# A gated recurrence with a causal gated unit: one store per chunk, and transfers in a searched order

## The chip, the cores and the metric

The kernel runs on one core of a Trainium2 chip. The metric is device time in microseconds (us), the median of the runs. The core has five engines with an instruction stream each: TensorE (PE), VectorE (DVE), ScalarE (ACT), GpSimd (POOL) and SyncE (SP, which here only issues loads). Sixteen DMA engines move data between HBM and the on-chip memory SBUF.

## The reference

The input has 4 sequences of 6336 tokens with 256 channels, in float32. A recurrence runs over the tokens, and its output feeds a gated unit whose gate is a causal convolution of 5 taps.

```python
# recurrence, c = 8
a_base = sigmoid(a_param)
a_t    = exp(c * sigmoid(r_gate) * log(clip(a_base, 1e-6, 1 - 1e-6)))
x_gated = sqrt(maximum(1 - a_t * a_t, 1e-6)) * sigmoid(i_gate) * x
for t in range(S):
    h = a_t[:, t] * h + x_gated[:, t]
    y[:, t] = h
# gated unit on y
gate_pre = sum over k of conv_w[k] * (y shifted by 4 - k tokens)
out = (sigmoid(gate_pre) * (y @ w_val)) @ w_out
```

x, r_gate, i_gate and the output have 26 MB each.

## The kernel before

The 25344 tokens are cut into 27 chunks, most of 1024 tokens (the first and two late ones 512, the last 256). For the convolution and what follows, a chunk is cut again into halves of 512. Each step of a chunk is a small function, and the text PLAN lists the steps in the order in which they are emitted, as name.chunk.half.PSUM-bank. Every engine executes its own steps in that order.

```python
NRI = 3     # buffers for the gates r and i
NX = 2      # buffers for x
NOSB = 5    # output buffers, half a chunk each
X_PE = [0, 1]   # chunks whose x goes through PE and DVE rather than POOL

PLAN = """
ldri.0.-1 ldri.1.-1 ldx.0.-1 ldx.1.-1 ldri.2.-1 ldw.-1 tanh.0.-1 srT.0.0.7 srT.0.1.5 exp.0.1.-1 exp.0.0.-1 e.0.0.-1
...
"""

def op_ldri(k, bank):                 # loads of both gates, on SP
    for e, src in ((0, rf), (1, if_)):
        nc.sync.dma_start(gate[:, slot(c, e), 0:n * H]..., toks(src, c, 0, n))
def op_ldx(k, bank):
    nc.sync.dma_start(xr[:, c % NX, 0:CHUNKS[c] // P, :], toks(xf, c, 0, CHUNKS[c]))
def op_tanh(k, bank):                 # ACT, both gates in one instruction, in place
    nc.scalar.activation(out=tgate[:, s0:s0 + 2, 0:w], in_=gate[:, s0:s0 + 2, 0:w], func=ACT.Tanh, scale=0.5)
# op_srT: PE transposes tanh(r/2); op_exp: ACT, a = exp(khf * t + khf) into aring
def op_e(k, bank):                    # POOL: a * a into ering
    nc.gpsimd.tensor_tensor(out=ering[...], in0=a, in1=a, op=ALU.mult)
def op_s1(k, bank):                   # POOL: 1 + tanh(i/2), in place in the i gate's buffer
    nc.gpsimd.tensor_scalar(out=t, in0=t, scalar1=1.0, scalar2=1.0, op0=ALU.add, op1=ALU.mult)
def op_u(k, bank):                    # POOL: u = (1 + tanh(i/2)) * x
    if c in X_PE: return op_ux(...)   # or on DVE, with x copied to PSUM by PE (op_xc)
    nc.gpsimd.tensor_tensor(out=u, in0=t, in1=xt, op=ALU.mult)
# op_sq: ACT, sqrt over one to three chunks, with another activation table
# op_nT: PE transposes the root; op_xg: DVE, u * root; op_xgT: PE transposes it
# op_scan: DVE, the recurrence; op_conv: PE, 5 taps; op_tg: ACT, tanh of the convolution
# op_val: PE, y @ w_val
def op_gv(k, bank):                   # DVE: (1 + tanh) * val
    nc.vector.scalar_tensor_tensor(out=gvr[:, nth[k] % NGV, :, 0:n], in0=tgr[...], scalar=1.0, in1=..., ...)
# op_out: PE, gv @ w_out into PSUM
def op_osbA(k, bank): nc.scalar.copy(out=dst, in_=src)            # PSUM to osb, on ACT
def op_osbD(k, bank): nc.vector.tensor_copy(out=dst, in_=src)     # or on DVE
def op_store(k, bank):                # one store per half chunk (512 KB), issued by ACT
    nc.scalar.dma_start(toks(of, c, o, n), osb[:, nth[k] % NOSB, 0:n // P * D]...)
```

DMAs signal completion through eight semaphores that the framework hands out in turn. A new transfer on a semaphore waits for the transfer that used it before.

Of the kernel before, what the change touches and what calls it, by code (L numbers as in the profile page):

```python
# [16 lines left out]
X_PE = [0, 1]  # L17
NRI = 3
NX = 2
# [4 lines left out]
NOSB = 5  # L24
NTG = 2
NGV = 2
# [7 lines left out]
ldri.0.-1 ldri.1.-1 ldx.0.-1 ldx.1.-1 ldri.2.-1 ldw.-1 tanh.0.-1 srT.0.0.7 srT.0.1.5 exp.0.1.-1 exp.0.0.-1 e.0.0.-1  # L34
tanh.1.-1 e.0.1.-1 xc.0.1.0 xc.0.0.6 ux.0.0.-1 xc.1.2.1 u.0.-1 sq.0.1.-1 ux.1.2.-1 srT.1.0.0 ldri.3.-1 xc.1.1.5
ldx.2.-1 nT.0.0.7 srT.1.1.4 exp.1.0.-1 xg.0.0.-1 ux.1.1.-1 exp.1.1.-1 xc.1.0.0 tanh.2.-1 xc.1.3.5 e.1.1.-1 ux.1.0.-1
e.1.0.-1 wc.-1 srT.2.0.3 s1.2.-1 srT.2.1.2 xgT.0.0.4 exp.2.0.-1 scan.0.0.-1 exp.2.1.-1 e.2.0.-1 u.1.-1 tanh.3.-1
ldx.3.-1 ldri.4.-1 e.2.1.-1 u.2.-1 srT.3.1.3 srT.3.0.6 xgT.0.1.1 sq.1.2.-1 s1.3.-1 ldx.4.-1 ldri.5.-1 nT.2.0.7
nT.2.1.0 u.3.-1 xg.2.0.-1 exp.3.1.-1 xg.2.1.-1 nT.1.1.7 scan.0.1.-1 nT.1.0.5 tanh.4.-1 xg.1.1.-1 conv.0.0.0 xg.1.0.-1
xgT.2.0.3 e.3.1.-1 ldx.5.-1 xgT.1.1.4 ldri.6.-1 xgT.1.0.2 scan.1.1.-1 tg.0.0.-1 exp.3.0.-1 s1.4.-1 srT.4.1.1  # L40
exp.4.1.-1 scan.1.0.-1 val.0.0.4 e.3.0.-1 tanh.5.-1 srT.4.0.6 gv.0.0.-1 conv.1.0.0 u.4.-1 scan.2.0.-1 xgT.2.1.7
tg.1.0.-1 srT.5.1.5 srT.5.0.4 exp.4.0.-1 scan.2.1.-1 val.1.0.0 exp.5.1.-1 e.4.1.-1 ldx.6.-1 ldri.7.-1 exp.5.0.-1
gv.1.0.-1 conv.2.0.6 tanh.6.-1 e.5.1.-1 out.0.0.4 conv.1.1.0 osbD.0.0.-1 e.4.0.-1 val.2.0.2 tg.1.1.-1 val.1.1.4
e.5.0.-1 store.0.0.-1 tg.2.0.-1 out.1.0.0 conv.2.1.6 osbD.1.0.-1 s1.5.-1 sq.3.3.-1 gv.1.1.-1 u.5.-1 gv.2.0.-1
out.2.0.0 out.1.1.4 osbD.2.0.-1 osbD.1.1.-1 s1.6.-1 nT.3.1.3 ldri.8.-1 nT.3.0.2 ldx.7.-1 val.2.1.0 tg.2.1.-1 xg.3.0.-1
xg.3.1.-1 store.1.0.-1 u.6.-1 tanh.7.-1 gv.2.1.-1 xgT.3.1.7 nT.4.0.6 scan.3.1.-1 srT.6.0.1 srT.6.1.4 xgT.3.0.2
nT.4.1.0 nT.5.1.5 exp.6.0.-1 xg.4.0.-1 s1.7.-1 ldri.9.-1 xg.4.1.-1 exp.6.1.-1 srT.7.0.1 xg.5.1.-1 ldx.8.-1 nT.5.0.6
scan.3.0.-1 exp.7.0.-1 out.2.1.4 e.6.1.-1 tanh.8.-1 xgT.4.1.3 srT.7.1.7 xg.5.0.-1 conv.3.0.0 e.7.0.-1 osbD.2.1.-1
scan.4.1.-1 conv.3.1.4 u.7.-1 store.1.1.-1 tg.3.0.-1 xgT.4.0.6 srT.8.0.2 tg.3.1.-1 scan.4.0.-1 srT.8.1.0 exp.7.1.-1
val.3.1.4 exp.8.1.-1 gv.3.1.-1 e.6.0.-1 conv.4.1.6 ldx.9.-1 exp.8.0.-1 ldri.10.-1 xgT.5.0.3 store.2.0.-1 tg.4.1.-1  # L50
out.3.1.4 e.7.1.-1 scan.5.0.-1 tanh.9.-1 xgT.5.1.7 val.3.0.0 e.8.0.-1 conv.4.0.2 gv.3.0.-1 osbD.3.1.-1 e.8.1.-1
tg.4.0.-1 scan.5.1.-1 val.4.1.4 s1.8.-1 val.4.0.0 sq.6.3.-1 out.3.0.2 gv.4.1.-1 u.8.-1 gv.4.0.-1 osbD.3.0.-1 out.4.0.0
out.4.1.2 osbD.4.0.-1 srT.9.1.6 osbD.4.1.-1 nT.8.1.5 s1.9.-1 ldri.11.-1 nT.6.1.4 xg.8.1.-1 exp.9.1.-1 conv.5.0.2
ldx.10.-1 xg.6.1.-1 store.3.0.-1 tanh.10.-1 e.9.1.-1 nT.6.0.4 nT.7.1.1 xg.6.0.-1 nT.7.0.0 xgT.6.1.5 xg.7.0.-1 u.9.-1
xgT.6.0.4 xg.7.1.-1 srT.9.0.6 scan.6.0.-1 nT.8.0.7 exp.9.0.-1 conv.5.1.0 tg.5.0.-1 scan.6.1.-1 tg.5.1.-1 xgT.7.1.2
s1.10.-1 ldri.12.-1 store.2.1.-1 tanh.11.-1 val.5.1.0 ldx.11.-1 xg.8.0.-1 srT.10.1.3 srT.10.0.6 gv.5.1.-1 e.9.0.-1
val.5.0.4 conv.6.1.0 gv.5.0.-1 exp.10.1.-1 u.10.-1 srT.11.1.7 scan.7.1.-1 store.3.1.-1 store.4.1.-1 conv.6.0.4
tg.6.1.-1 exp.10.0.-1 srT.11.0.1 xgT.7.0.0 tg.6.0.-1 val.6.0.2 scan.7.0.-1 exp.11.0.-1 e.10.0.-1 out.5.0.4 ldri.13.-1
store.4.0.-1 ldx.12.-1 exp.11.1.-1 osbD.5.0.-1 out.5.1.0 e.10.1.-1 tanh.12.-1 conv.7.0.6 osbD.5.1.-1 e.11.0.-1
val.6.1.4 gv.6.0.-1 gv.6.1.-1 out.6.0.2 tg.7.0.-1 e.11.1.-1 store.5.1.-1 osbD.6.0.-1 xgT.8.1.6 xgT.8.0.7 s1.11.-1  # L60
out.6.1.4 scan.8.1.-1 sq.9.3.-1 val.7.0.2 u.11.-1 gv.7.0.-1 osbD.6.1.-1 conv.7.1.2 scan.8.0.-1 srT.12.0.1 srT.12.1.6
nT.9.0.0 nT.9.1.4 s1.12.-1 ldri.14.-1 nT.11.0.5 xg.9.0.-1 exp.12.0.-1 nT.10.0.7 ldx.13.-1 xg.9.1.-1 store.6.1.-1
xg.11.0.-1 store.5.0.-1 tg.7.1.-1 xgT.9.1.0 e.12.0.-1 scan.9.1.-1 exp.12.1.-1 out.7.0.2 tanh.13.-1 val.7.1.4 u.12.-1
osbD.7.0.-1 conv.8.0.0 gv.7.1.-1 nT.10.1.2 xgT.9.0.3 xg.10.1.-1 tg.8.0.-1 srT.13.0.6 scan.9.0.-1 s1.13.-1 ldri.15.-1
store.7.0.-1 tanh.14.-1 val.8.0.0 ldx.14.-1 out.7.1.4 xg.10.0.-1 e.12.1.-1 conv.8.1.2 gv.8.0.-1 srT.13.1.7 osbD.7.1.-1
store.6.0.-1 tg.8.1.-1 u.13.-1 xgT.10.0.1 srT.14.0.0 scan.10.0.-1 exp.13.0.-1 srT.14.1.4 out.8.0.2 exp.14.0.-1
xgT.10.1.6 store.7.1.-1 osbD.8.0.-1 exp.13.1.-1 conv.9.0.0 e.14.0.-1 exp.14.1.-1 scan.10.1.-1 ldx.15.-1 val.8.1.2
ldri.16.-1 tg.9.0.-1 nT.11.1.7 val.9.0.4 e.13.0.-1 store.8.0.-1 tanh.15.-1 gv.8.1.-1 conv.9.1.0 gv.9.0.-1 e.14.1.-1
out.8.1.2 val.9.1.4 osbD.8.1.-1 tg.9.1.-1 e.13.1.-1 xg.11.1.-1 store.8.1.-1 gv.9.1.-1 xgT.11.0.3 out.9.0.0 s1.14.-1
sq.12.3.-1 scan.11.0.-1 out.9.1.6 xgT.11.1.5 u.14.-1 osbD.9.1.-1 osbD.9.0.-1 val.10.0.6 srT.15.1.4 scan.11.1.-1  # L70
conv.10.0.2 s1.15.-1 nT.12.1.1 ldri.17.-1 tg.10.0.-1 nT.12.0.0 xg.12.1.-1 ldx.16.-1 srT.15.0.5 exp.15.1.-1 xg.12.0.-1
conv.10.1.2 gv.10.0.-1 u.15.-1 exp.15.0.-1 xgT.12.0.0 val.10.1.6 scan.12.0.-1 tg.10.1.-1 nT.13.1.1 store.9.0.-1
tanh.16.-1 conv.11.0.4 gv.10.1.-1 nT.13.0.3 e.15.0.-1 ldri.18.-1 nT.14.0.0 xg.13.1.-1 out.10.1.6 ldx.17.-1 xg.14.0.-1
xg.13.0.-1 tg.11.0.-1 e.15.1.-1 srT.16.0.2 osbD.10.1.-1 out.10.0.0 tanh.17.-1 val.11.0.6 osbD.10.0.-1 s1.16.-1
xgT.12.1.3 gv.11.0.-1 srT.16.1.1 conv.11.1.4 u.16.-1 scan.12.1.-1 exp.16.1.-1 val.11.1.6 tg.11.1.-1 srT.17.1.0
exp.16.0.-1 gv.11.1.-1 xgT.13.0.5 srT.17.0.4 store.10.0.-1 exp.17.1.-1 conv.12.0.2 scan.13.0.-1 e.16.0.-1 ldri.19.-1
store.9.1.-1 exp.17.0.-1 nT.14.1.0 ldx.18.-1 xgT.13.1.7 tg.12.0.-1 xg.14.1.-1 e.17.1.-1 scan.13.1.-1 store.10.1.-1
tanh.18.-1 out.11.0.2 xgT.14.0.4 e.16.1.-1 conv.12.1.0 osbD.11.0.-1 val.12.1.6 scan.14.0.-1 e.17.0.-1 tg.12.1.-1
out.11.1.2 val.12.0.0 s1.17.-1 gv.12.1.-1 sq.15.3.-1 gv.12.0.-1 out.12.1.6 u.17.-1 osbD.11.1.-1 out.12.0.4
osbD.12.1.-1 xgT.14.1.2 val.13.0.0 osbD.12.0.-1 conv.13.0.6 scan.14.1.-1 s1.18.-1 srT.18.0.3 ldri.20.-1 srT.18.1.5  # L80
tg.13.0.-1 nT.16.1.4 ldx.19.-1 store.12.0.-1 exp.18.1.-1 nT.17.0.2 gv.13.0.-1 u.18.-1 conv.13.1.6 store.11.0.-1
store.11.1.-1 exp.18.0.-1 xg.16.1.-1 nT.15.1.5 xg.17.0.-1 nT.15.0.1 tg.13.1.-1 xg.15.1.-1 val.13.1.2 xg.15.0.-1
tanh.19.-1 out.13.0.4 gv.13.1.-1 e.18.1.-1 ldri.21.-1 xgT.15.0.1 osbD.13.0.-1 conv.14.0.6 ldx.20.-1 scan.15.0.-1
e.18.0.-1 store.12.1.-1 tg.14.0.-1 srT.19.0.5 nT.17.1.0 exp.19.0.-1 nT.16.0.7 s1.19.-1 val.14.0.2 xg.17.1.-1
tanh.20.-1 xg.16.0.-1 xgT.15.1.5 gv.14.0.-1 srT.19.1.1 u.19.-1 scan.15.1.-1 out.13.1.2 xgT.16.0.7 exp.19.1.-1
srT.20.1.0 osbD.13.1.-1 srT.20.0.6 exp.20.1.-1 conv.14.1.4 scan.16.0.-1 exp.20.0.-1 e.19.0.-1 out.14.0.2 ldx.21.-1
ldri.22.-1 tg.14.1.-1 val.14.1.0 osbD.14.0.-1 e.19.1.-1 tanh.21.-1 xgT.16.1.5 conv.15.0.6 gv.14.1.-1 conv.15.1.2
e.20.1.-1 scan.16.1.-1 xgT.17.0.4 tg.15.1.-1 e.20.0.-1 scan.17.0.-1 tg.15.0.-1 srT.21.0.5 val.15.0.0 s1.21.-1
out.14.1.2 gv.15.0.-1 sq.18.3.-1 val.15.1.6 osbD.14.1.-1 s1.20.-1 srT.21.1.4 out.15.0.0 gv.15.1.-1 osbD.15.0.-1
u.20.-1 xgT.17.1.7 conv.16.0.2 scan.17.1.-1 store.13.0.-1 nT.18.1.1 nT.18.0.0 nT.19.1.6 xg.18.1.-1 tg.16.0.-1  # L90
nT.20.1.7 xg.18.0.-1 u.21.-1 ldri.23.-1 store.13.1.-1 exp.21.1.-1 val.16.0.2 xg.19.1.-1 xg.20.1.-1 ldx.22.-1 nT.20.0.1
store.14.0.-1 exp.21.0.-1 gv.16.0.-1 nT.19.0.6 xgT.18.0.7 store.15.0.-1 tanh.22.-1 xg.20.0.-1 out.15.1.4 xg.19.0.-1
conv.17.0.2 scan.18.0.-1 ldri.24.-1 conv.16.1.0 tg.17.0.-1 osbD.15.1.-1 s1.22.-1 xgT.18.1.7 store.14.1.-1 tg.16.1.-1
srT.22.1.2 scan.18.1.-1 xgT.19.0.3 exp.22.1.-1 out.16.0.0 e.21.0.-1 tanh.23.-1 val.16.1.4 osbD.16.0.-1 srT.22.0.2
# [412 lines left out]
```

## Time and profile before

| What | Value |
|---|---|
| Device time, median of 3 runs | 310.14 us (310.02 to 310.45) |
| Span of the profiled execution | 309.0 us |
| HBM read, written | 78.39 MB, 25.95 MB |
| Loads to landing, 1 MB, median | r 11.7 us, i 9.6 us, x 10.0 us |
| Stores to landing, 512 KB, median | 7.9 us |
| ACT: gate tanh, 23 full chunks | 83.4 us busy, 3626 ns each |
| ACT: PSUM copies, 9 | 8.7 us busy |
| DVE: recurrence, 46 full halves of channels | 106.9 us busy, 2337 ns each |
| DVE: PSUM copies, 41 | 49.0 us busy, 1211 ns each |
| POOL: u, 22 full chunks | 90.6 us busy, 4120 ns each |

In a profile line, an entry such as "L345 POOL ... uring<-gate,xr" names the line of the kernel, the engine, and what is written and read. "pp" is PSUM, "osb" the output buffers, "gate" the gate buffers. A wait line names who waited, for whom, the total, the number of times and the longest. A slice digit is the busy share in tenths of one fortieth of the span.

### The profile page before, as it was taken

What the parts mean: (1) busy time and instruction counts of PE and PEld (TensorE: products, weight loads), DVE (VectorE), ACT (ScalarE), POOL (GpSimd) and SP (SyncE); (2) the same over time, 40 slices, a digit from 0 to 9 for tenths busy, and PEclk for the clock granted to TensorE, in tenths of its full rate; (3) what the DMA queues carried; (4) which work ended last, traced back from release to release, by engine and by line L of the source; (5) the groups of instructions that cost most, each with busy time, mean ns of one, the idle gap of its engine ahead of it and who ended that gap; (6) DMA issues with size and microseconds to landing.
All of it is one profiled execution on the core that took longest, in us unless ns stands there. A gap on an engine that the chain in (4) does not pass through costs nothing.

```text
span 309.0 us, 6335 instructions
## 1 busy us (share of the span) xinstructions
PE 248.1 (80%) x2627; PEld 167.7 (54%) x2627; DVE 252.3 (82%) x208; ACT 278.5 (90%) x185; POOL 235.2 (76%) x118
## 2 busy tenths in 40 slices
PE   0582577958888898799489998988899987999994
PEld 0232454447546564557257665675666655565763
DVE  1052079479898989999499999999999998989893
ACT  6799999999999999998699999999999979868632
POOL 3229998997998999899996799989959993038000
PEclk9995589999999999999979999999999999999999
DMA  7999999998997999999999997999897764182555
GB/s 288 427 360 422 382 417 364 365 352 318 389 377 263 413 414 422 421 421 421 428 423 365 363 390 280 376 426 424 336 369 309 285 249 137 69 337 109 200 212 237
DMA packets 19466, 104.74 MB, mean 339 GB/s; under 512 B 2151, under 2 KB 2670, under 8 KB 10606
## 3 DMA queue, kind: packets, MB, share of 16 engines
q1 hardware_dynamic: 12224, 78.39, 65.0%
q10 hardware_dynamic: 7214, 25.96, 21.0%
q8 instruction: 20, 0.33, 0.4%
q14 instruction: 8, 0.07, 0.1%
HBM read 78.39 MB, written 25.95 MB: 338 GB/s over the span
## 4 chain that ended last, share of the span: by engine, by line
PE 24%; DMA 21%; POOL 18%; ACT 17%; issue 11%; DVE 6%; ACTq 1%; SPq 1%; POOLq 0%; DVEq 0%
DMA gate<-in_i_gate_dram 13%; POOL uring L345 10%; PE pp L407 7%; PE pp L439 6%; DMA xr<-in_x_dram 6%; ACT gate L290 5%; POOL ering L310 5%; ACT tgr L417 4%; PE pp L425 4%; ACT aring L304 4%; POOL gate L318 3%; PE pp L367 3%; DMA out_dram<-osb 3%; DVE yring L395 3%; PE pp L327 2%
## 5 line engine op out<-in xcount | busy, mean ns | idle before, releaser
L310 POOL TENSOR_TENSOR ering<-aring 128x1024 f32<-128x1024 f32 (+2 forms) x54 | 93.6, 1754 | 36.7 <-ACT aring L304 35.1
L395 DVE TENSOR_TENSOR_SCAN yring<-aring,yring,pp 128x1024 bf16<-128x1024 f32 (+2 forms) x52 | 113.4, 2193 | 4.1 <-PE pp L382 4.1
L345 POOL TENSOR_TENSOR uring<-gate,xr 128x2048 bf16<-128x2048 bf16 (+2 forms) x25 | 96.0, 3845 | 4.3 <-PE pp L382 2.6
L290 ACT ACTIVATE gate<-gate 128x4096 bf16<-128x4096 f32 (+2 forms) x27 | 90.2, 3340 | 7.6 <-DMA xr<-in_x_dram 3.9
L407 PE MATMUL pp<-yring,diag 64*64 64x512 bf16 (+13 forms) x1224 | 65.3, 341 | 5.2 <-DVE yring L395 2.2
L430 DVE SCALAR_TENSOR_TENSOR gvr<-tgr,pp 128x1024 bf16<-128x1024 bf16 (+1 forms) x50 | 59.4, 1200 | 8.9 <-ACT tgr L417 6.7
L439 PE MATMUL pp<-wo,gvr 128*128 128x256 bf16 x396 | 52.7, 279 | 13.9 <-DVE gvr L430 7.9
L304 ACT ACTIVATE aring<-pp,khf 128x1024 f32<-128x1024 bf16 (+2 forms) x54 | 59.3, 1144 | 3.9 <-PE pp L295 2.2
L417 ACT ACTIVATE tgr<-pp 128x1024 bf16<-128x1024 f32 (+1 forms) x50 | 50.5, 1024 | 10.0 <-PE pp L407 8.6
L439 PEld LDWEIGHTS <-gvr 128*128 128x128 bf16 x396 | 42.5, 115 | 23.8 <-DVE gvr L430 11.1
L425 PE MATMUL pp<-yring,wv 128*128 128x512 bf16 (+1 forms) x200 | 50.5, 377 | 6.1 <-DVE osb L454 2.2
L454 DVE COPY osb<-pp 128x1024 f32<-128x1024 f32 x41 | 49.0, 1211 | 6.1 <-PE pp L439 5.9
L318 POOL TENSOR_SCALAR gate<-gate 128x2048 bf16<-128x2048 bf16 (+2 forms) x25 | 44.5, 1781 | 5.4 <-ACT gate L290 5.4
L407 PEld LDWEIGHTS <-diag 64*64 64x64 bf16 x1224 | 30.6, 107 | 30.6 <-issue 14.5
L354 ACT ACTIVATE ering<-ering,b 128x4096 bf16<-128x4096 f32 (+4 forms) x16 | 46.4, 2932 | 0.1
L374 DVE TENSOR_TENSOR uring<-uring,pp 128x1024 bf16<-128x1024 bf16 (+1 forms) x50 | 32.0, 672 | 12.7 <-PE pp L367 12.5
L295 PE MATMUL pp<-ident_b,gate 128*128 128x128 bf16 x396 | 31.4, 229 | 13.2 <-ACT gate L290 11.1
L295 PEld LDWEIGHTS <-gate 128*128 128x128 bf16 x396 | 26.6, 103 | 21.9 <-ACT gate L290 14.0
L367 PE MATMUL pp<-ident_f,ering 128*128 128x128 f32 x198 | 32.3, 303 | 5.4 <-ACT ering L354 3.9
L382 PE MATMUL pp<-ident_f,uring 128*128 128x128 f32 x198 | 31.5, 282 | 6.1 <-ACT tgr L417 2.8
L367 PEld LDWEIGHTS pp<-ident_f,ering 128*128 128x128 f32 x198 | 27.8, 208 | 11.6 <-ACT ering L354 4.8
L425 PEld LDWEIGHTS <-wv 128*128 128x128 bf16 x200 | 18.8, 98 | 23.9 <-issue 11.1
(33 smaller groups left out, 86.9 us busy)
## 6 DMA issues: line engine op xcount, KB each, us to landing
out_dram<-osb ACTq DMA_DIRECT2D x49, 512.0 KB, 7.9
gate<-in_r_gate_dram SPq DMA_DIRECT2D x23, 1024.0 KB, 11.7
gate<-in_i_gate_dram SPq DMA_DIRECT2D x23, 1024.0 KB, 9.6
xr<-in_x_dram SPq DMA_DIRECT2D x23, 1024.0 KB, 10.0
gate<-in_r_gate_dram SPq DMA_DIRECT2D x3, 512.0 KB, 7.7
gate<-in_i_gate_dram SPq DMA_DIRECT2D x3, 512.0 KB, 10.7
xr<-in_x_dram SPq DMA_DIRECT2D x3, 512.0 KB, 3.4
yring<-in_moe_w_val_dram SPq DMA_DIRECT2D x1, 256.0 KB
```

Source lines behind the costliest of these rows:

```text
L290: nc.scalar.activation(out=tgate[:, s0:s0 + 2, 0:w], in_=gate[:, s0:s0 + 2, 0:w], func=ACT.Tanh, scale=0.5)
L295: nc.tensor.transpose(out=ppb[:, bank * 2 * BANK + j * P:bank * 2 * BANK + (j + 1) * P], in_=tgate[:, slot(c, 0), j * D + h * P:j * D + (h ...
L304: nc.scalar.activation(out=dst, in_=src, func=ACT.Exp, scale=khf[:, h:h + 1], bias=khf[:, h:h + 1])
L310: nc.gpsimd.tensor_tensor(out=ering[:, c % NE, h * n:(h + 1) * n], in0=a, in1=a, op=ALU.mult)
L345: nc.gpsimd.tensor_tensor(out=u, in0=t, in1=xt, op=ALU.mult)
L367: nc.tensor.transpose(out=pp[:, d0:d0 + P], in_=src[:, w, :], identity=ident_f[:])
L395: nc.vector.tensor_tensor_scan(out=yring[:, h, y0:y0 + n], data0=aring[:, c % NA, h, 0:n], data1=src, initial=prev, op0=ALU.mult, op1=ALU.add)
L407: nc.tensor.matmul(out=pp[col * HP:(col + 1) * HP, b0 + d0:b0 + d1], lhsT=diag[r * HP:(r + 1) * HP, h, kk, :], rhs=yring[r * HP:(r + 1) * ...
L417: nc.scalar.activation(out=tgr[:, nth[k] % NTG, :, 0:n], in_=two(live["conv", k], n), func=ACT.Tanh, scale=0.5)
L425: nc.tensor.matmul(out=pp[:, (bank + m) * BANK:(bank + m) * BANK + n], lhsT=wv[:, hk, m, :], rhs=yring[:, hk, y0:y0 + n], start=(hk == 0), ...
L430: nc.vector.scalar_tensor_tensor(out=gvr[:, nth[k] % NGV, :, 0:n], in0=tgr[:, nth[k] % NTG, :, 0:n], scalar=1.0, in1=two(live["val", k], n ...
L439: nc.tensor.matmul(out=pp[:, bank * BANK + j * D:bank * BANK + (j + 1) * D], lhsT=gvr[:, nth[k] % NGV, m, 0:n].rearrange("c (p q) -> c q p ...
```

## The change

Stores and buffers: a store now covers a whole chunk (1 MB), from two output buffers of a full chunk. The gated product is written in place over the tanh, which has three buffers; its own buffers are gone. The memory goes to a third x buffer. It is meant to make fewer, larger transfers and to let x loads start earlier.

Order: the gate loads of a chunk are separate steps (ldr, ldi), and PLAN is a new order in which the sequence of all transfers was searched together with the eight semaphores. Ordering edges between successive transfers keep this sequence, so that the semaphores fall as planned. The edges order emission only and add no wait on the chip.

Start: r of chunk 0 has a tanh of its own; x of chunks 0 and 1 goes through POOL like all others; the casts of the weights move from ACT to POOL; the logarithm is taken of 1 + exp(-a) and clamped afterwards.

```diff
-X_PE = [0, 1]
+X_PE = []
-NX = 2
+NX = 3
-NOSB = 5
-NTG = 2
-NGV = 2
+NOSB = 2
+NTG = 3
... (PLAN is replaced as a whole)
-    with tc.manual_schedule():
+    with tc.manual_schedule(engines={SP, Activation, DVE, PE}):   # POOL: kept in program order
-        osb = rings.tile([P, NOSB, SUBN // P * D], FP32, name="osb")
+        osb = rings.tile([P, NOSB, CMAX // P * D], FP32, name="osb")
-        gvr = rings.tile([P, NGV, H, SUBN], BF16, name="gvr")
+        def dma(queue, dst, src):
+            i = queue.dma_start(dst, src)
+            if turn:
+                tc.add_manual_dep(i.ins, turn[-1].ins.name,
+                                  mybir.DependencyInfo(mybir.DependencyClass.NoSync, mybir.DependencyReason.DATA),
+                                  reason="turn of the transfers")
+            turn.append(i)
... (all transfers go through dma; op_ldri becomes op_ldr and op_ldi)
-        nc.scalar.dma_start(wrow[:], moe_conv_w[:, :])
+        nc.scalar.preload_act_table_set("natural_log_exp_and_others")
+        dma(nc.scalar, wrow, moe_conv_w[:, :])
-        nc.vector.tensor_scalar(out=ksig[:], in0=kex[:], scalar1=1.0, scalar2=None, op0=ALU.add)
-        nc.vector.reciprocal(out=ksig[:], in_=ksig[:])
... 
-        nc.scalar.activation(out=kln[:], in_=ksig[:], func=ACT.Ln)
+        nc.scalar.activation(out=kln[:], in_=kex[:], func=ACT.Ln, bias=1.0)
...
         def op_wc(k, bank):
-                nc.scalar.copy(out=wv[...], in_=wvf[...])
-            nc.scalar.activation(out=wo2[:], in_=wof, func=ACT.Copy, scale=0.5)
+                keep(nc.gpsimd.tensor_scalar(out=wv[...], in0=wvf[...], scalar1=1.0, scalar2=1.0, ...))
+            keep(nc.gpsimd.tensor_scalar(out=wo2[:], in0=wof, scalar1=0.5, scalar2=1.0, ...))
...
+        def op_tanhi(k, bank):      # used for chunk 0; op_tanh takes only r there
+            nc.scalar.activation(out=tgate[:, slot(c, 1), 0:w], in_=gate[:, slot(c, 1), 0:w], func=ACT.Tanh, scale=0.5)
...
-            nc.vector.scalar_tensor_tensor(out=gvr[:, nth[k] % NGV, :, 0:n], in0=tgr[...], ...
+            nc.vector.scalar_tensor_tensor(out=tgr[:, nth[k] % NTG, :, 0:n], in0=tgr[...], ...
...
         def op_store(k, bank):
-            nc.scalar.dma_start(toks(of, c, o, n), osb[:, nth[k] % NOSB, 0:n // P * D]...)
+            dma(nc.scalar, of[start[c]:start[c] + n, :].rearrange("(m p q) d -> p m (q d)", m=m, q=q),
+                osb[:, c % NOSB, 0:n * H].rearrange("p (m w) -> p m w", m=m))
```

## The prediction

> **What bounds the kernel now.** I read the table of engines first, then the span in slices, then the same span cut where ScalarE's job changes, then ScalarE's timeline where it pauses, then the waits of the load queue.
>
> ```profile
> PE 248.1 (80%) x2627; PEld 167.7 (54%) x2627; DVE 252.3 (82%) x208; ACT 278.5 (90%) x185; POOL 235.2 (76%) x118
> ...
> ACT  6799999999999999998699999999999979868632
> ...
> DMA  7999999998997999999999997999897764182555
> ```
>
> ACT is the busiest engine, and the slices show that its 10% of idle time lies in three places: the first two slices, one dip near the middle, and the last seven. DMA is full for most of the first three quarters and half empty at the end. I cut the span at 5.75 us (the first gate tanh starts), 21 us (start-up over) and 265.78 us (the last gate tanh, of chunk 26, starts). The columns of the next view are the stretch, its length, then busy time and instructions of each engine, clock, DMA share and GB/s.
>
> ```profile
> 0.00:5.75 5.75, 0.61 (x3) 0.46 (x3) 1.13 (x7) 2.94 (x4) 1.52 (x8) 1.00 0.68 239
> 5.75:21.00 15.25, 10.03 (x39) 5.15 (x40) 3.57 (x6) 12.98 (x9) 2.84 (x3) 1.00 1.04 403
> 21.00:265.78 244.78, 199.01 (x2134) 137.53 (x2138) 212.34 (x167) 237.13 (x147) 220.62 (x99) 0.96 0.92 363
> 265.78:309.00 43.22, 38.41 (x460) 24.55 (x452) 35.30 (x30) 25.40 (x28) 10.19 (x9) 0.99 0.49 196
> ```
>
> From 5.75 to 265.78 us (260.0 us) ACT is busy 12.98 + 237.13 = 250.1 us, so it pauses only 9.9 us: ACT sets the time there. In the last 43.2 us PE is busy 38.4 us and ACT 25.4: there PE sets it, finishing convolutions and output products that have piled up. So the span is 5.75 + 250.1 + 9.9 + 43.2 = 309.0 us, and I predict each term again.
>
> The largest pause of ACT is here:
>
> ```profile
> 144.80 1.07 ACT L417 ACTIVATE tgr<-pp 128x1024 bf16<-128x1024 f32 x1
> 149.31 0.34 ACTq L459 DMA_DIRECT2D out_dram<-osb  x1
> 149.78 3.62 ACT L290 ACTIVATE gate<-gate 128x4096 bf16<-128x4096 f32 x1 [3.90 <-DMA xr<-in_x_dram]
> 152.03 0.34 ACTq L459 DMA_DIRECT2D out_dram<-osb  x1
> ```
>
> A store stands in ACT's instruction stream; it is issued only when an x load has landed, and ACT idles 3.90 us behind it. A store has no data in common with an x load. They share a semaphore: the built program has eight for DMAs, and a transfer waits for the last user of its own. The waits of the load queue say the rest:
>
> ```profile
> SPq L220 <- POOL uring L345: 88.7, 12, 13.7
> SPq L224 <- POOL uring L345: 73.0, 9, 18.4
> ...
> SPq L220 <- PE pp L295: 26.5, 6, 8.9
> SPq L224 <- DMA xr<-in_x_dram: 17.5, 5, 6.0
> ```
>
> Loads mostly wait for POOL's product u, which frees an i gate buffer and an x buffer; some 30 us are waits for other transfers. From 100 to 160 us the same table gives 420 GB/s, from 50 to 100 us only 341: supply is full in one stretch and held back before it.
>
> **What the Trainium skill says.** "Perfetto Trace Analysis", section "Optimization Strategy", says to take the most-contended engine of each regime and ask what ends its gaps; the trace agrees that there are two regimes here (ACT 96% busy, then PE 89%). "DMA: Bandwidth & Descriptors", section "Anatomy of one DMA", says that DMA engines wait on no semaphores: the wait happens on the issuing sequencer. The 3.90 us above agree: the wait of a store stopped ACT. The same page, section "Issuing engines are not separate DMA queues", says that DMAs of all issuers interleave on the same 16 engines. The trace agrees: from 100 to 160 us loads took 73.2% and stores 27.8%, and a 512 KB store needed a median of 9.7 us to land. "ScalarE: Activation LUTs", section "What ACT_TABLE_LOAD costs", gives 1283 ns a load plus a drain of about 1380 ns; 22 loads took 1283 ns each here, but the drain doesn't show (load at 14.35 us, square root at 15.64).
>
> **The change part by part.** I count from the built instruction order of both kernels.
>
> *Start.* Before, the first tanh reads both gates of chunk 0. Now r has its own tanh, and ln(1 + e) replaces an add, a reciprocal and a clamp on DVE between exp and ln (0.64 us of waiting). The first table is asked for before the second small DMA rather than after both. Exp ended at 3.07 us and ln began at 3.71, so the second table load can end at about 4.5 instead of 5.21 us, and r of chunk 0 alone should have landed by then. First term: 4.6 us, 1.15 less.
>
> *ACT's work up to the last gate tanh.* Gone: three weight casts, now on POOL (0.69 + 0.63 = 1.3 us), and one 512-wide exp (0.8), which comes later. Added: tanh of chunk 0 in two halves (2 x 1.05 instead of 1.91, +0.2); three more PSUM copies, 4 instead of 1 (3 x 1.01 = 3.0); two more gate tanhs, 41 instead of 39 (2 x 1.03, starts 0.92 to 1.0 apart, 2.0). The table loads stay 22. Net +3.1: 250.1 becomes 253.2 us. So the change does not relieve ACT; over the whole kernel it does 14 copies instead of 9. DVE gets the relief: 36 copies instead of 41 (5 x 1.21 = 6.1 us) and no ux products (4.2).
>
> *ACT's pauses.* The old 9.9 us are 2.3 in start-up, 1.1 from 21 to 50 us, 4.4 from 100 to 150 (mostly the store), 1.6 from 250 to 266, and scraps. In the new start-up I expect 0.3 for the transposes of chunk 0, 0.8 for POOL's two squares (2 x 1.04) before the first square root, and 0.3 for the i gate of chunk 3, some 1.5 us; POOL takes on u and (1+tanh) of chunks 0 and 1 and the casts, about 11 us, but it idled 16.6 of the first 21 us. After it, each transfer waits for the one eight before it. With 1 MB stores there are 113 transfers instead of 136, so eight cover more bytes, and the order was chosen so that the eighth before is old: for instance the x load of chunk 13 waits for store 4, which stands 8.7 us of ACT work earlier in the order. The third x buffer lets an x load go one chunk earlier. I leave 2.5 us for what no plan foresees: 4.0 in all.
>
> *The tail.* After the last gate tanh PE has one convolution (1.21 us), one output product (0.87), one value product (0.86) and one n transpose group (0.25) less, and one transpose group of r (0.3) and of xg (0.44) more: 2.4 less. DVE has two gated products, two copies and one xg product less (5.4). PE's 38.4 become 36.0, and with about 4.2 of its old 4.8 us of idle time the tail is 40.2.
>
> Sum: 4.6 + 253.2 + 4.0 + 40.2 = 302.0 us of span. The median before is 310.14 for a span of 309.0, so I add some 0.7 and predict 302.7 us.
>
> *Bytes* don't change. A store still writes 4 KB per descriptor run (four tokens), so its efficiency per byte stays: loads took 65.0% for 78.39 MB and stores 21.0% for 25.96 MB, 0.83 and 0.81% per MB. 104.74 MB at the 420 GB/s of the full stretch are 249 us; the loads end well before the tail, so that is a floor below, not the bound.
>
> **The rivals.** *Two output buffers become the bound.* Before, five buffers of 512 KB; a copy waits for the store five halves back. Now a copy of chunk c waits for the whole store of chunk c-2. Counting ACT work in the order between a store and the first copy into its buffer, the median falls from 11.6 to 6.9 us and the least is 2.2 (store 8, copy of chunk 10; DVE has 3.6 us of other work there). A 1 MB store beside loads should take at least the 7.9 us median of the old 512 KB, by my estimate 8 to 11. DVE is the second busiest engine, 143 of 150 us between 100 and 250 us, so such waits would reach PE and then ACT: half of 24 reuses at 1 us would cost 10 us, and the time would be 310 to 313. Against it: DVE has 10 us less to do, and whoever ordered the transfers placed stores for this.
>
> *The load stream was the true bound.* The chain of waits between 105 and 152 us runs through loads and a store, 8 to 9 us each. If supply set the pace, smoother supply would repay more than ACT's pauses: but ACT is the floor directly above it, so no better than 4.6 + 253.2 + 1 + 38.5 = 297.3 of span (38.5 is a tail in which PE idles 2.5 us).
>
> *POOL becomes the bound.* POOL must do about 238 us before the last gate tanh from about 7.5 us on, leaving some 14 us of slack. It speaks against, unless a late u holds the loads; then 306.
>
> **Range and chances.** The floor of 297.3 and about half of the first rival's loss (308) bound the range: 297.5 to 308. The 2% line is 303.9, only 1.2 us above my number, so faster gets 0.62, within 2% gets 0.33, slower 0.05.
>
> **What would show each step.** First gate tanh at 4.6 us; last one near 261.8 with ACT busy 253 between; copies to osb on ACT 14; no multi-microsecond gap of ACT before a store; the tail near 40 us with PE busy 36. I am wrong if DVE copies wait for stores, if a store landing takes over 10 us and shows in DVE's waits, or if ACT's pauses stay near 10 us under new names.

## The result, and the profile after

The changed kernel takes 343.55 us in the median (343.27 to 344.95) against 310.19 us for the kernel before on the same chips: a ratio of 1.108, with a 95% interval of 1.105 to 1.112. It is 33 us slower, where 302.7 us was predicted.

The page of the changed kernel: busy time of each engine, then the busy share of ACT and DMA in forty slices.

```profile
PE 253.3 (74%) x2615; PEld 173.7 (51%) x2615; DVE 244.9 (72%) x195; ACT 284.0 (83%) x188; POOL 245.4 (72%) x125
...
ACT  7889999998895876949999859969988993987943
...
DMA  7999999568997799978997899499991295263345
```

No engine has much more to do than before. ACT went from 278.5 to 284.0 us, POOL, which took over the casts and two products u, from 235.2 to 245.4, and DVE from 252.3 to 244.9; what grew is idle time, spread over the whole span (the 5, 7, 6 and 4 of ACT), and DMA now has holes in the first three quarters. So it is not a dearer operation but waiting. The cuts made of before, at the same events (first gate tanh at 4.39 us, last one at 300.51), with the same columns: stretch, length, busy time and instructions of PE, PEld, DVE, ACT and POOL, clock, DMA share, GB/s:

```profile
0.00:4.39 4.39, 0.23 (x1) 0.17 (x1) 0.62 (x4) 2.94 (x5) 1.06 (x7) 1.00 0.52 178
4.39:21.00 16.61, 6.60 (x49) 5.29 (x53) 3.19 (x4) 14.47 (x11) 12.57 (x11) 1.00 1.03 409
21.00:300.51 279.51, 211.35 (x2153) 144.95 (x2146) 209.85 (x161) 240.53 (x146) 224.69 (x101) 0.95 0.82 320
300.51:341.50 40.99, 35.16 (x422) 23.26 (x419) 31.23 (x27) 26.06 (x29) 7.05 (x7) 0.97 0.46 187
```

ACT's work between the two events is 14.47 + 240.53 = 255.0 us, its pauses 300.51 - 4.39 - 255.0 = 41.1 us, the tail 41.0 us. The pauses were 9.9 us before. They are nearly the whole loss: 31.2 of the 32.5 us by which the span grew. The table of waits says for whom the engines waited (total, times, longest):

```profile
ACT gate L301 <- DMA gate<-in_i_gate_dram: 18.2, 8, 4.2
...
POOL uring L361 <- DMA xr<-in_x_dram: 17.6, 4, 9.0
...
DVE osb L472 <- DMA out_dram<-osb: 14.4, 4, 7.3
...
ACT aring L320 <- PE pp L311: 10.9, 11, 5.0
...
ACT aring L320 <- DMA out_dram<-osb: 5.4, 1, 5.4
```

Four of these five lines end with a transfer: an i gate load that ACT waits for, an x load that POOL waits for, and stores. DVE waits for stores before it may copy into their buffer. In the last line ACT stands behind a store in its own stream, issued at 286.29 us, which waits for an earlier store with the same semaphore to land. This wait comes from no shared buffer: it is there, with 4.3 us, in the version below whose copies wait for no store too. Before, DVE's copies waited for PE alone, and ACT for i gates 3.6 us:

```profile
L454 DVE COPY osb<-pp 128x1024 f32<-128x1024 f32 x41 | 49.0, 1211 | 6.1 <-PE pp L439 5.9
```

```profile
ACT gate L290 <- DMA gate<-in_i_gate_dram: 3.6, 4, 1.6
```

The chain of waits of the changed kernel between 78 and 146 us shows how they follow one another (start, length, what):

```profile
78.63 15.13 DMA xr<-in_x_dram
...
93.92 4.13 POOL uring L361
...
98.07 8.55 DMA gate<-in_i_gate_dram
...
106.78 3.63 ACT gate L301
...
121.30 9.99 DMA gate<-in_i_gate_dram
...
131.47 13.40 DMA out_dram<-osb
...
145.00 1.24 DVE osb L472
```

An x load lands late, so POOL's u is late, so the i gate buffer that u frees is late, so the next i load and ACT's tanh are late. Further down a copy waits for a store of 13.4 us, which ACT issued only when the tanh that had waited for its i gate was under way. Why the x load started only at 78 us is seen in the timeline of the load queue (start, length, queue, transfer, number):

```profile
63.68 4.39 SPq L218 DMA_DIRECT2D gate<-in_i_gate_dram  x2
68.42 0.33 SPq L218 DMA_DIRECT2D gate<-in_r_gate_dram  x1
77.75 0.33 SPq L218 DMA_DIRECT2D gate<-in_i_gate_dram  x1
78.17 2.49 SPq L218 DMA_DIRECT2D xr<-in_x_dram  x3
```

The three x loads at 78.17 us are those of chunks 9, 7 and 8. The buffers of 7 and 8 had been free since u of chunks 4 and 5 ended (63.6 and 67.7 us). They stood in the queue behind the i load of chunk 9, which had to wait for u of chunk 6 (77.7 us). From 75 to 78 us the DMA engines moved 8 GB/s, and from 77.75 to 84 us six loads went out.

### The profile page after: what moved, and what is told of

Same layout as the page of the kernel before. It is cut to its first block, busy times and chain, and to the rows that moved or that the text cites. A ratio compares the mean times of both kernels' runs of the same rounds, so it can differ in the third digit from the quotient of the medians.

```text
span 341.5 us, 6267 instructions
## 1 busy us (share of the span) xinstructions
PE 253.3 (74%) x2615; PEld 173.7 (51%) x2615; DVE 244.9 (72%) x195; ACT 284.0 (83%) x188; POOL 245.4 (72%) x125
## 4 chain that ended last, share of the span: by engine, by line
DMA 38%; PE 19%; ACT 12%; DVE 11%; POOL 11%; issue 7%; SPq 2%; ACTq 0%; POOLq 0%; DVEq 0%
DMA xr<-in_x_dram 16%; DMA out_dram<-osb 11%; DMA gate<-in_i_gate_dram 11%; POOL uring L361 8%; PE pp L423 6%; DVE yring L411 5%; PE pp L383 4%; ACT ering L370 4%; PE pp L398 2%; PE pp L311 2%; PE pp L455 2%; DVE uring L390 2%; ACT aring L320 2%; ACT gate L301 2%; PE pp L441 2%
## 5 line engine op out<-in xcount | busy, mean ns | idle before, releaser
L361 POOL TENSOR_TENSOR uring<-gate,xr 128x2048 bf16<-128x2048 bf16 (+2 forms) x27 | 102.0, 3787 | 32.0 <-DMA xr<-in_x_dram 17.6
L301 ACT ACTIVATE gate<-gate 128x4096 bf16<-128x4096 f32 (+2 forms) x27 | 89.1, 3301 | 20.2 <-DMA gate<-in_i_gate_dram 18.2
L446 DVE SCALAR_TENSOR_TENSOR tgr<-tgr,pp 128x1024 bf16<-128x1024 bf16 (+1 forms) x50 | 59.3, 1202 | 32.8 <-PE pp L441 23.0
L423 PE MATMUL pp<-yring,diag 64*64 64x512 bf16 (+11 forms) x1224 | 68.7, 352 | 12.3 <-ACT aring L320 4.7
L455 PE MATMUL pp<-wo,tgr 128*128 128x256 bf16 x396 | 52.7, 282 | 9.2 <-ACT tgr L433 3.3
L472 DVE COPY osb<-pp 128x1024 f32<-128x1024 f32 x36 | 43.2, 1217 | 21.6 <-DMA out_dram<-osb 14.4
L455 PEld LDWEIGHTS <-tgr 128*128 128x128 bf16 x396 | 42.8, 116 | 18.9 <-issue 9.1
L423 PEld LDWEIGHTS <-diag 64*64 64x64 bf16 x1224 | 33.3, 110 | 37.3 <-issue 22.7
L311 PE MATMUL pp<-ident_b,gate 128*128 128x128 bf16 x396 | 34.5, 239 | 22.5 <-ACT gate L301 17.6
L334 POOL TENSOR_SCALAR gate<-gate 128x2048 bf16<-128x2048 bf16 (+2 forms) x27 | 47.2, 1756 | 2.7 <-ACT gate L301 2.7
L383 PE MATMUL pp<-ident_f,ering 128*128 128x128 f32 x198 | 35.6, 327 | 18.2 <-ACT ering L370 14.0
```

What stands on the lines that cost most here:

```text
L301: nc.scalar.activation(out=tgate[:, s0:s1, 0:w], in_=gate[:, s0:s1, 0:w], func=ACT.Tanh, scale=0.5)
L311: nc.tensor.transpose(out=ppb[:, bank * 2 * BANK + j * P:bank * 2 * BANK + (j + 1) * P], in_=tgate[:, slot(c, 0), j * D + h * P:j * D + (h ...
L361: keep(nc.gpsimd.tensor_tensor(out=u, in0=t, in1=xt, op=ALU.mult))
L383: nc.tensor.transpose(out=pp[:, d0:d0 + P], in_=src[:, w, :], identity=ident_f[:])
L423: nc.tensor.matmul(out=pp[col * HP:(col + 1) * HP, b0 + d0:b0 + d1], lhsT=diag[r * HP:(r + 1) * HP, h, kk, :], rhs=yring[r * HP:(r + 1) * ...
L446: nc.vector.scalar_tensor_tensor(out=tgr[:, nth[k] % NTG, :, 0:n], in0=tgr[:, nth[k] % NTG, :, 0:n], scalar=1.0, in1=two(live["val", k], n ...
```

## The experiments

Four theories were on record, the last of them after the first four runs. A: the order of the loads in their one queue. B: the two output buffers. C: the new compute order is itself worse. D: in that order gate tanhs come sooner than their loads can, since a gate load cannot start before POOL's u frees the buffer. All ratios are against the kernel before on the same chip. Where some executions of a version fell in a slower state, its time, like its ratio, is that of the others.

### One part undone at a time

*Loads in ascending order.* The loads from chunk 3 or 4 on are taken out of PLAN and put back in the order r, i, x, chunk by chunk, each right after the last reader of its buffer. Nothing else moves.

```diff
-store.2.-1 ldi.9.-1 ldx.9.-1 ... store.3.-1 ldx.7.-1 ldx.8.-1 ldr.10.-1 ldr.11.-1 u.7.-1
+osbD.2.0.-1 u.4.-1 ldi.7.-1 ldx.7.-1 ldr.8.-1 ...
```

> Only the order of the loads is changed: from chunk 4 on (x from chunk 3 on) they come as r, i, x in ascending order of chunks, each emitted right after the last reader of its buffer; compute order, buffers and stores are those of the changed kernel. Theory A (in the searched order loads stand in the one load queue behind loads that wait for POOL, so gates and x arrive late): ACT's waits for gate loads (20 us) and POOL's for x (17.6 us) mostly go, the time falls to 312 to 322. Theory B (two output buffers hold the copies, and those hold PE and ACT): 335 or more, as DVE's waits for stores remain. Theory C (the compute order itself is worse, whatever the transfers do): 335 or more, with the pauses of ACT on PE.

Measured: 329.9 us, ratio 1.063 (1.060 to 1.067), 4.5 points below the changed kernel, or 14 us. That is short of what A alone expected, and more than B or C allowed. POOL's waits for x went from 17.6 to 1.4 us. ACT's waits for i gates went only from 18.2 to 13.7, where A had most of them go, and the copies still wait:

```profile
DVE osb L471 <- DMA out_dram<-osb: 10.1, 4, 4.7
...
POOL uring L360 <- DMA xr<-in_x_dram: 1.4, 1, 1.4
```

With the order of the loads the hand-out of the eight semaphores changes too: the load queue waited 34.9 us for stores in the changed kernel and 7.7 us here. How much of the 14 us is this, and how much the loads standing behind one another, no run separates.

*Copies that wait for no store.* Every copy goes to a buffer that no store reads, and every store reads zeros of the same size. The output is left out; work and traffic stay.

```diff
-            return osb[:, c % NOSB, q0 * D:(q0 + q) * D], pp[...]
+            return osb[:, 1, q0 * D:(q0 + q) * D], pp[...]
-                osb[:, c % NOSB, 0:n * H]...   # the store
+                osb[:, 0, 0:n * H]...          # zeros
```

> The copies go to one buffer that no store reads, and every store reads another buffer that is written once with zeros (so the output is left out); transfers, their sizes and their order are those of the changed kernel. So a copy never waits for a store, and a store for no copy. Theory A: 14 us of DVE waits go, but loads stay late: 331 to 340. Theory B: 315 to 325. Theory C: 335 or more.

Measured: 332.4 us, 1.071 (1.068 to 1.074), some 11 us below the changed kernel. The time lies in A's range and not in B's, so the buffers are not all of it. ACT's waits for i gates stayed at 16.4 us and POOL's for x at 16.2, so they are a cause beside the first.

*Both.*

> Both edits together: loads in ascending order, and copies that no store holds (the output is left out). Theories A and B together leave only the work of ACT, the start and the tail, with the 4 us of pauses of the prediction: 300 to 308. Theory C: 320 or more, as the compute order is the same.

Measured: 323.2 us, 1.041 (1.036 to 1.046). The two parts gave 4.5 and 3.8 points, both together 6.7 rather than 8.3: two causes that overlap in part. 13 us are left, and the time lies in C's range, so C was still open.

*Half-chunk stores.* The load order of the changed kernel stays, but its 16 KB of output buffer are four halves, each with a 512 KB store as before.

```diff
-NOSB = 2
+NOSB = 4
-        osb = rings.tile([P, NOSB, CMAX // P * D], FP32, name="osb")
+        osb = rings.tile([P, NOSB, SUBN // P * D], FP32, name="osb")
```

> The changed kernel with its loads in the searched order, but the stores undone: one store of 512 KB per half chunk from four buffers of half a chunk (the same memory), each issued by ACT five steps of the plan after its copy. Theory A: 333 to 345, the loads are as late as before. Theory B: 318 to 328, the waits of the copies for stores go from 14 us to under 5. A rival to both: more transfers put the semaphores out of step, and it is slower than 344.

Measured: 333.4 us, 1.075 (1.072 to 1.078). In the same memory, two small stores beat one large one by 10 us, and DVE's waits for stores are gone. Still the time lies in A's range and not in B's: ACT's waits for i gates grew from 18.2 to 22.6 us, and the load queue's waits for stores from 34.9 to 63.5, with 50 stores instead of 27 on the same eight semaphores. I read the gain so (no run tests it alone, and the stores stand in other places of the order as well): with one store per chunk, the first half of a buffer stays taken until the second half is copied and both are stored.

*No ordering edges.*

```diff
-            if turn:
+            if False:
```

> The changed kernel without the ordering edges between transfers; the same order on every engine, but the framework hands out the semaphores in another sequence. If the searched fit of the semaphores is worth anything, it gets slower, 350 or more; theories A, B and D give semaphores little part: 338 to 349.

Measured: 336.4 us, 1.084 (1.078 to 1.090), faster than with the edges. The load queue of the changed kernel waited 34.9 us for stores, 6 times:

```profile
SPq L218 <- POOL uring L361: 168.4, 21, 21.3
...
SPq L218 <- DMA out_dram<-osb: 34.9, 6, 9.7
```

Without the edges the second line is gone from its table, while POOL's waits for x (14.7 us) and the copies' waits for stores (16.5 us) stay. So the searched fit of semaphores is no gain here; it costs 2.4 points. The edges are no waits themselves, but they decide which transfers share a semaphore, and so which of them wait for one another.

### How much an output buffer is worth

*The old compute order in the changed kernel's memory.* PLAN of before, three x buffers, ascending loads, free copies (output left out). Three tanhs move by up to six places for the shared tanh buffers.

```diff
 PLAN of before, with ldri split, one store per chunk, loads re-placed
+X_PE = [0, 1]
```

> The compute order of the kernel before (three tanh steps moved by up to six places, x of chunks 0 and 1 on PE) in the frame of the changed kernel: three x buffers, product in place, 1 MB stores, loads in ascending order, and copies that no store holds (the output is left out). To be compared with 322 us, the same frame with the new compute order. Theory C or D (the new compute order costs the rest): 300 to 308. If frame and traffic cost the rest: 315 or more.

Measured: 312.6 us, 1.010 (1.007 to 1.012), between the two ranges. No gain from the third x buffer shows in the old order. Against the 323.2 us of the new order in the same frame, the new order loses 10 us.

*The same with a real output*, 512 KB stores from four half buffers; five stores move ahead.

```diff
-NOSB = 2      # whole chunks, copies free
+NOSB = 4      # half chunks, read by the stores
```

> A complete kernel: compute order of before, start-up of the change (r of chunk 0 first, casts on POOL), three x buffers, loads in ascending order, stores of 512 KB from four half buffers. If two output buffers, the load order and the new compute order are what hurt, this keeps the good parts: 303 to 309, a little faster than before. If three x buffers or ascending loads are themselves no gain: 309 to 315.

Measured: 334.9 us, 1.081 (1.076 to 1.086): 20 us above the higher of the two ranges. I had looked for the best of both kernels and overlooked that its output had four half buffers where before has five.

*Before, with four half buffers.* To see whether one buffer can be worth that much, the kernel before loses one; five stores have to move ahead with it.

```diff
-NOSB = 5
+NOSB = 4
 PLAN: store.2.1, 13.0, 16.0, 17.0 and 17.1 stand 1 to 33 places earlier
```

> The kernel before with four 512 KB output buffers instead of five; five stores stand a few places earlier so that each still comes before the copy that reuses its buffer. Nothing else changes, and the memory freed is left unused. Theory B (output buffering is what costs): the loss of 25 us that the version with the old order and real half-chunk stores showed against the one with free copies must be found here too: 318 to 340 us, with DVE's copies waiting for stores (before: none). Rival: that loss belonged to the rest of that version (the third x buffer, which lets more loads into the queues beside the stores): then four buffers cost at most a few us, 310 to 314.

Measured: 336.7 us, 1.086 (1.081 to 1.091). A single 512 KB buffer is worth 27 us (by the ratio) to the kernel before. Its waits:

```profile
DVE osb L454 <- DMA out_dram<-osb: 26.4, 9, 4.2
...
ACT tgr L417 <- PE pp L407: 20.0, 10, 5.8
...
ACT aring L304 <- PE pp L295: 10.9, 7, 4.2
```

None of the three was over 9 us before (none, 8.6, 2.2). DVE stops at a copy, PE then stops for DVE, ACT for PE, and the total comes out at the end almost undiminished, though DVE was only 82% busy before. The median store got no slower for it (7.7 us, before 7.9). The moved stores explain little: a store moved too far ahead would hold ACT until its copy is done, but ACT's waits for copies of DVE come to 2.3 us.

*Three output buffers instead of three x buffers*, in the changed kernel, with ascending loads and its real output.

```diff
-NX = 3
+NX = 2
-NOSB = 2
+NOSB = 3
```

> The changed kernel with its 12 spare KB moved back: two x buffers and three 1 MB output buffers, loads in ascending order (r and i of chunk c, then x of chunk c-1). Compute order, 1 MB stores, start-up as in the changed kernel. Theory B with A: the third x buffer buys nothing and a third output buffer frees the copies, so the time comes near the version with ascending loads and free copies, 320 to 327 us. Rival: x loads held back by two buffers cost what the copies gain: 330 to 336 us, as with the ascending loads alone.

Measured: 326.3 us, 1.051 (1.047 to 1.056), in the range of B with A, and 3.6 us below the ascending loads alone. DVE waited for no store. The memory that the change gave to x was of more use to the output.

### What is left of the compute order

*An eighth of x.* From the version with both parts undone, only an eighth of each x is loaded from chunk 4 on: 20 MB of traffic less, and the output is left out.

```diff
-            dma(nc.sync, xr[:, c % NX, 0:CHUNKS[c] // P, :], toks(xf, c, 0, CHUNKS[c]))
+            w = CHUNKS[c] // P if c < 4 else 1
+            dma(nc.sync, xr[:, c % NX, 0:w, :], toks(xf, c, 0, CHUNKS[c])[:, 0:w, :])
```

> As the run with ascending loads and free copies (322 us), but from chunk 4 on only an eighth of x is loaded (the rest of the x buffer keeps old data, so the product u is wrong, and the output is left out): 20 MB of 105 less traffic, every instruction of the engines unchanged. Theory D (in this compute order a gate load may start only when POOL's u has freed its buffer, and ACT's tanh comes earlier than a 1 MB load beside other traffic lands): gate loads land sooner, ACT's 12 us of waits for i gates fall under 4, the time falls to 306 to 313. Theory C (the order of POOL, PE and ACT itself waits): 318 to 323.

Measured: 312.3 us, 1.008 (1.005 to 1.011): 11 us for less traffic with the same instructions. D expected the time; a bad compute order (C) would have kept it. But ACT's waits for i gates fell only from 12.2 to 7.9 us, where D had said under 4, and a lighter DMA load helps any theory of transfers, so gate buffers were tried directly.

*A fourth gate buffer, on both orders.* The third x buffer goes, and since no store reads a copy, the output shrinks to 4 KB of zeros and 4 KB for the copies.

```diff
-NRI = 3
+NRI = 4
-NX = 3
+NX = 2
-                osb[:, 0, 0:n * H].rearrange(...)
+                osb[:, 0, 0:n * H // m].unsqueeze(1).to_broadcast([P, m, n * H // m])
```

> The changed compute order with ascending loads and copies that wait for no store (323.2 us so far), and a fourth gate buffer: the third x buffer goes, and as no store reads a copy, the output buffers shrink to 4 KB of zeros, which every store reads, and 4 KB for the copies (the output is left out). Gate loads may start a whole chunk earlier. Theory D: ScalarE's waits for gate loads (12.2 us) go and the time falls by about as much, to 309 to 315 us. Theory C: the waits go and the time stays, 319 to 326 us, because ScalarE then waits for TensorE instead.

> The control: the old compute order in the same frame with four gate buffers (312.6 us with three). Its ScalarE waited 3.0 us for gate loads, so a fourth buffer can give at most about that: 308 to 313 us. If it falls as far as the changed order does, the fourth buffer is a help to any order and the 10 us between the two stay unexplained.

Measured: the new order falls from 323.2 to 309.7 us, 0.999 (0.997 to 1.001); the old one only from 312.6 to 311.5, 1.005 (1.003 to 1.007). First the waits of the new order with three gate buffers, then with four:

```profile
ACT gate L301 <- DMA gate<-in_i_gate_dram: 12.2, 7, 3.6
```

```profile
ACT gate L301 <- DMA gate<-in_i_gate_dram: 2.5, 1, 2.5
```

With three, the chain shows the reason: the i load starts when u ends, and takes as long as the traffic makes it.

```profile
112.11 4.07 POOL uring L361
116.20 12.91 DMA gate<-in_i_gate_dram
```

So C falls: with loads in time the new order is as good as the old. It asks for a fourth gate buffer, for which there is no memory beside the rest.

### All causes removed at once, with the real output

Giving up one of five buffers of a squared leaves room for two x, three output, three r and four i gate buffers in the same 202 KB. It took three steps.

```diff
-NX = 3, NOSB = 2, NE = 5
+NX = 2, NOSB = 3, NE = 4, NI = 4      # r and i gates in rings of their own
-            return 2 * (c % NRI) + e
+            return NRI + c % NI if e else c % NRI
```

> The changed kernel, whole output, its compute order, 1 MB stores and start-up unchanged, with the memory dealt otherwise: two x buffers, three 1 MB output buffers, three r and four i gate buffers, and four instead of five buffers of a squared; loads in ascending order. If the three causes make up the loss, it comes to the time of the version with four gate buffers and free copies, 308 to 314 us, that is level with before. If some cause is still missing, or four buffers of a squared hold POOL or ScalarE back, 318 us or more.

Measured: 430.6 us, 1.394 (1.389 to 1.398), missed by far. The load queue's waits:

```profile
SPq L218 <- PE pp L312: 231.6, 21, 26.4
```

Again a fault in the order of the loads, now mine: each r load, whose buffer is freed by a late transpose, stood ahead of an x and an i load whose buffers had long been free.

```diff
-ldr.9.-1 ldx.7.-1 ldi.9.-1      # by chunk
+ldx.7.-1 ldi.9.-1 ldr.9.-1      # by the time their buffers come free
```

> The same kernel as the one that took 430 us (whole output, two x, three output, three r and four i gate buffers), with the loads sorted by when their buffer comes free in the compute order, so that no load stands behind one whose buffer is freed later. If the order of the loads alone was the fault: 308 to 316 us, level with before. If the four buffers of a squared hold the engines back: 330 us or more still.

Measured: 408.3 us, 1.321 (1.316 to 1.327). Missed too, so that order cost 22 us and was not the main fault. Its waits:

```profile
ACT gate L302 <- DMA gate<-in_i_gate_dram: 43.7, 8, 10.9
...
ACT gate L302 <- DMA gate<-in_r_gate_dram: 35.0, 7, 9.1
```

One tanh reads r and i of a chunk. With rings of different length these lie apart, the tanh takes a strided slice, and it waits for up to five transfers instead of two. I read it so: all that lies between the two buffers is taken as read and written. The load queue fits this, as loads wait for the tanh here (0.8 us in the changed kernel):

```profile
SPq L218 <- ACT gate L302: 49.5, 7, 10.9
```

Two tanhs mend that:

```diff
-            nc.scalar.activation(out=tgate[:, s, 0:w], in_=gate[:, s, 0:w], ...)   # s = slice(s0, s1 + 1, s1 - s0)
+            nc.scalar.activation(out=tgate[:, slot(c, 0), 0:w], in_=gate[:, slot(c, 0), 0:w], ...)
+            nc.scalar.activation(out=tgate[:, slot(c, 1), 0:w], in_=gate[:, slot(c, 1), 0:w], ...)
```

> The kernel of 408 us with the one tanh over r and i of a chunk, whose two buffers lie apart there, divided into one for r and one for i, so that each waits for its own load alone. The second tanh costs ScalarE about 0.2 us a chunk (2 x 1.06 instead of 1.91 in chunk 0), some 5 us in all. If the wide waits were the fault and the three causes are all there are: 311 to 319 us, and no wait of ScalarE for an r load. If four buffers of a squared, or a fourth cause, hold it back: 330 us or more.

Measured: 311.6 us, 1.005 (1.003 to 1.006). Its cuts, at its first and last r tanh:

```profile
0.00:4.48 4.48, 0.23 (x1) 0.18 (x1) 0.62 (x4) 2.94 (x4) 1.05 (x7) 1.00 0.48 186
4.48:21.00 16.52, 6.80 (x55) 5.25 (x56) 3.19 (x4) 15.21 (x13) 12.87 (x11) 0.98 1.02 405
21.00:271.58 250.58, 200.77 (x2120) 139.52 (x2143) 208.07 (x161) 240.50 (x170) 224.30 (x101) 0.95 0.89 357
271.58:311.70 40.12, 34.77 (x415) 23.11 (x418) 31.32 (x27) 26.06 (x30) 7.06 (x7) 0.99 0.50 195
```

Pauses are 271.58 - 4.48 - 255.7 = 11.4 us instead of 41.1, with work (255.7) and tail (40.1) as in the changed kernel. Compute order, whole-chunk stores, start-up and edges are those of the change, so buffers, load order and gate loads make up its loss, and the edges cost nothing visible in this order. A wait of 8.2 us for r loads is new, against the expectation. No version was faster than before.

### The new start-up alone

Before, with r of chunk 0 in a tanh of its own, ln(1 + e), and the first table asked for earlier.

```diff
+        nc.scalar.preload_act_table_set("natural_log_exp_and_others")
         nc.scalar.dma_start(wrow[:], moe_conv_w[:, :])
-        nc.scalar.activation(out=kln[:], in_=ksig[:], func=ACT.Ln)
+        nc.scalar.activation(out=kln[:], in_=kex[:], func=ACT.Ln, bias=1.0)
```

> The kernel before with only the new start-up: r of chunk 0 has a tanh of its own, ln(1 + e) replaces three small operations, the first table is asked for before the second small transfer. Expected if the start was sized rightly: the first tanh 1.2 to 1.4 us earlier, of which 0.2 is given back by the second half of that tanh: 308.8 to 309.6 us, about 1 us faster than before. Rival: ACT then waits for later loads of the start-up instead: no change.

Measured: 310.1 us, 1.001 (1.000 to 1.003): no gain. ACT's timeline at the start, with what each instruction waited for:

```profile
4.35 1.06 ACT L287 ACTIVATE gate<-gate 128x1024 bf16<-128x1024 f32 x1
5.59 1.06 ACT L292 ACTIVATE gate<-gate 128x1024 bf16<-128x1024 f32 x1 [0.18 <-DMA gate<-in_i_gate_dram]
6.55 1.44 ACT L306 ACTIVATE aring<-pp,khf 128x512 f32<-128x512 bf16 x2
10.85 3.62 ACT L287 ACTIVATE gate<-gate 128x4096 bf16<-128x4096 f32 x1 [2.86 <-DMA gate<-in_i_gate_dram]
```

The first tanh does start 1.4 us earlier (5.75 before), and ACT gives it back in front of the tanh of chunk 1, at 10.85 us (10.71 before): that one waits for its load either way.

## Why the prediction was wrong, point by point

*Start, 4.6 us:* 4.39 us; the step was right. In the kernel before it would have been worth nothing, as the last run shows: the next load sets the time there.

*ACT's work, 253.2 us:* 255.0 us; right within 2 us.

*The tail, 40.2 us with PE busy 36:* 41.0 us with PE busy 35.2; right.

*ACT's pauses, "4.0 in all":* 41.1 us. This is the step that failed: the term of the sum that I mis-sized, by 37 of the 41 us between prediction and result. It asked of each transfer only whether the one eight before it, with the same semaphore, had landed; the runs show waits for buffers in its place, and beside them a 5.4 us wait of ACT behind a store, where the prediction had named the absence of such gaps as a sign. Three sentences of it did not hold:

- "The order was chosen so that the eighth before is old." I took a searched order on trust and looked at the semaphores only, not at the order of the loads among themselves. In one queue a load that waits for its buffer holds every load behind it. "DMA: Bandwidth & Descriptors", section "Anatomy of one DMA", which I had quoted, says where a DMA's wait happens, on the issuing sequencer; the 168.4 us that SP waits here for POOL's u agree with it. That sum alone shows no fault, as it was 161.7 us before; the fault is what stands behind the wait, as the two x loads with free buffers did until 78 us. Ascending loads gave 14 us, the change of semaphores that they bring included.
- "The third x buffer lets an x load go one chunk earlier." It could, and the order made no use of it; with the old order in ascending loads no gain shows either (312.6 us). It took its memory from the output.
- "I leave 2.5 us for what no plan foresees." The order puts gate tanhs where a load of 8 to 13 us (8.55, 9.99 and 12.91 in the chains above), issued when u ends, cannot have landed: 13 us, gone with a fourth gate buffer.

*The rival of two output buffers* was named and its sign was right; it was dismissed with "whoever ordered the transfers placed stores for this". The estimate, half of 24 reuses at 1 us, is 12 us, put down as 10; free copies gave 11. That the size fits is luck in part: DVE did not wait some twelve times for 1 us but four times for 14.4 us in all. What failed was the discounting; of the 10 us less that DVE was to have to do, the page shows 7.4. The trace of before held a better number than my count of ACT work. Set the first copy of each chunk against the landing of the last store two chunks back, as both stand in that trace (the issue where no landing is recorded): in 14 of 25 chunks the copy comes first, by up to 16.7 us. Three chunks back, it comes first in none of 24. For 15 of the 50 stores no landing is recorded, so these are the least counts. It is the difference between two and three output buffers in one view, before either ran; of the load order it says nothing. The same check shows how close to the edge before stood: set against the store five half chunks back, every copy comes after the landing, but the closest by 0.1 us; four back, 11 of 46 copies come first. One half buffer less cost 27 us.

*The load stream as the true bound* was kept as a rival that could only bring gain. It was nearer the truth, on the side I left out: a floor of 249 us for the bytes says nothing of when each load may start. *POOL as the bound* did not come: POOL is 72% busy and waits for loads. Its work before the last gate tanh, 238.3 us, is what was counted; the slack put down as 14 us is 16 by the prediction's own terms.

*The range* was built from the rivals one by one, each at most 10 us. The runs show three causes that add up for the most part, each moving the same chain.

## What to carry to other kernels

Before output buffers are merged or given away, set each copy against the landing of the store whose buffer it would take, from the trace at hand; a ring that just covers the landings, here by 0.1 us at the closest, shows no wait at all until one buffer is gone. In an in-order load queue, sort the loads by when their buffers come free; a load that must wait costs all those behind it. Ask of a new compute order not how busy its engines are but when the last reader of each buffer ends and whether the next load fits between that and its use.

## What the runs showed of the hardware that was not expected

With one half buffer less, waits passed through three engines almost without loss: 26.4 us of DVE at stores became a span 24.8 us longer (309.0 to 333.8), though the engine that sets the time, ACT, was not the one that waited. In the changed kernel less came through: of 14.4 us of such waits, free copies gave back 9.4 us of span (341.5 to 332.1).

How long a store took to land depended on more than its size. 1 MB stores had medians from 4.8 us (the 408 us version) to 11.3 us (the old order with free copies), 512 KB stores from 4.7 us (half-chunk stores) to 7.9 us (before). With the loads in the searched order it was 7.6 us for 1 MB and 4.7 us for 512 KB. The longest 1 MB store of the changed kernel took 13.7 us.
